# Pacing the side queue of a fused attention and feed-forward kernel: a constant number of queued jobs a step, gaps that end a step, and a later place for a partner's transposes

## The chip, the cores and the metric

The kernel runs on one core of one Trainium2 chip. The metric is the device time in microseconds (us). Each run is one execution of the whole program; runs of two kernels are compared on the same chip.

## The reference

Attention with root-mean-square normalised queries and keys, then a two-layer feed-forward block with a squared ReLU. All data are float32 (the weights arrive as float64 words).

```python
batch, n_heads, seq, head_dim = (8, 12, 448, 64)
n_tokens, d_model, d_ff = (3584, 768, 2048)

def rmsnorm(x, g):
    rms = np.sqrt(np.mean(x * x, axis=-1, keepdims=True) + 1e-06)
    return x / rms * g
q_n, k_n = rmsnorm(q, g_q), rmsnorm(k, g_k)
scores = 1.0 / np.sqrt(head_dim) * np.matmul(q_n, k_n.transpose(0, 1, 3, 2))
scores = scores - np.max(scores, axis=-1, keepdims=True)
attn = np.exp(scores)
attn = attn / (np.sum(attn, axis=-1, keepdims=True) + 1e-09)
x = np.matmul(attn, v)                  # (B, H, S, D)
x = x.transpose(0, 2, 1, 3).reshape(batch * seq, n_heads * head_dim)
h = np.maximum(x @ w_in, 0.0)
out = h * h @ w_out
```

## The kernel before

**Work and units.** The 96 heads are 48 pairs of two heads, six pairs to a batch element; the code numbers them i = 0 to 47. The feed-forward block runs over two batch elements at a time, so there are four units, `ffn(0)` to `ffn(3)`. Its products are formed with sums of blocks (fewer products, more additions): `first_products` (L961) in the first unit, `deep_products` (L995) in the others, and `second_products` (L1148) in all. While the products of a unit run on TensorE (PE), the attention of the pairs for the next unit is laid between them. The pairs up to 12 have no products beside them (`visit_alone`).

**Streams, steps and places.** `ffn` is a generator: each `yield` ends a step and gives its cost. Costs are 18 for a first product (6 matrix instructions), 30 or 10 in the second products of the first unit (4 instructions for 10), and 9 or 6 for deep products and 10 or 20 for second products later. `run(until)` (L1504) takes steps from the stream until the sum of costs, `spent`, reaches a place that `place(u, x)` gives. Then a visit to a pair follows. In the first unit a pair has two visits (`visit_among`, here called 14.0 and 14.1 for pair 14), 83.67 cost units apart. From pair 25 on a pair has one visit (`visit_whole`), at the places 99, 321 and 451 of each block of 481 units. Pair 25 is visited after the first unit has been drained, pair 37 after the second.

**What a visit does.** On PE it multiplies weights and values of the pair before (`attend`) and scores of this pair (`score`); ScalarE (ACT) makes exponentials from the scores (`weigh`, L453). An even pair's last score, `score(i, NJ)`, uses the transposed q and k of pair i + 1 also, its partner. All engines work through their instructions in the order of issue, which is the order in which this program's Python code runs.

**The side queue.** Small jobs that must be done between visits stand in two queues, `tasks` and `pool_tasks`. At the end of each step `run` calls `run_tasks(most, ...)`, with most = 2 for a cost above 10 and 1 otherwise; `run_tasks` (L1523) takes `most + len(some) // 5` jobs from the front of each queue. A visit begins with `run_all`, which empties both. In the later units some stretches of a block hold a queue back (`held`). The jobs are:

- for a coming pair, put in by `prepare` (L1665): room for squares; for x = 0 (q) and x = 1 (k), `square` (L172, ACT, into the same room) and `rows.add` (L191, a sum on VectorE, DVE, at L193 and a scaling at L196); then `put_in_order`, whose `rescale` runs on GpSimd (POOL: a power at L203, and a scaling of q at L218), with `store_q` and `load_blocks` (L325), which bring q, and k, back by blocks of 32 through DRAM;
- for the next pair, put in half way between two visits: `turn_blocks(i + 1, x)` (L363), a DVE transpose at L366 and, for q, a scaling on ACT at L368; and `load_qk(i + 4)`;
- after a visit: `invert`, `finish` or `invert_both` (divisions by the sums of weights, on DVE and POOL), and in `pool_tasks` six additions of weights (`add_up`, L472, POOL).

A `lambda: None` in the queue takes up the place of one job. In odd whole visits, jobs that were made by `partial` for this i (the turns of pair i + 1 and the load) are taken out before `run_all` as `late`, and put back to the front of the queue after the visit.

**Beside it.** In the same steps, `make_sum` (L1426) makes forms of the weights in turn on DVE and POOL (L1432), `convert` makes float32 weights from words (ACT L1319 to L1321, DVE L1332 to L1356), `deep_steps` derives and stores forms (L1392, L1410), and `follow_plan` makes forms of the attention's results (L718). DMAs of pairs go through a list, `transfers`, of which some are issued in each step (`follow_transfers`), all on the queue of SyncE (SP). When not in the first unit, `run_all` issues all that are left. `load_piece` (L879) brings in_sb, the weights of the deep products, from in_deep.

Of the kernel before, what the change touches and what calls it, by code (L numbers as in the profile page):

```python
# [224 lines left out]
def program(ctx, tc, rows, v, g, wide, ones, moe_w_in, moe_w_out, out, shift):  # L225
# [78 lines left out]
    def in_blocks(i):  # L304

        return 1 < i < len(pairs) and not alone(i - 2) and not shift
# [14 lines left out]
    def follow_transfers(most):  # L321
        for _ in range(min(len(transfers), most)):
            key, to, some = transfers.popleft()
            if to is not None:
                nc.sync.dma_start(to, some)  # L325
# [6 lines left out]
    def store_q(i):  # L332

        if not i % 2:
            through[i // 2] = dram.tile([2, S, 2 * D], F32, name="q_rows", tag="q_rows", bufs=2)
        to, queue = through[i // 2], transfers_of("q", i)
        queue.dma_start(
            to[i % 2, 0 : NJ * P].rearrange("(j p) c -> p j c", p=P),
            rows.part(i, 0)[:, 0:NJ].rearrange("p j h d -> p j (h d)"),
        )  # L340
        if not i % 2:
            for odd in range(2):
                queue.dma_start(
                    to[odd, NJ * P : S],
                    rows.room(i)[ds(odd * D, D), 0, NJ].rearrange("p h d -> p (h d)"),
                )

    def load_blocks(i, x):
        b, c = pairs[i]
        if x == 0 and slowly:  # L350
            while any(some[0][0] == "q" for some in list(transfers)[-4:]):
                transfers.append((("blocks", i, x), None, None))
        for e in range(2):
            source = through[i // 2][i % 2, :, ds(e * D, D)] if x == 0 else rows.qk[1][b, 2 * c + e]
            for half in range(2):
                transfers_of("blocks", i, x).dma_start(
                    room_for_blocks(i, x)[ds(e * D + half * SIDE, SIDE)].rearrange(
                        "p (t n) -> p t n", n=SIDE
                    ),
                    source[:, ds(half * SIDE, SIDE)].rearrange("(t p) n -> p t n", p=SIDE),  # L360
                )
# [26 lines left out]
    def rescale(i, x):  # L388
        ensure("qk", i)
        rows.power(i, x)  # L390
        if x == 0 or shift:
            rows.scale(i, x, nc.gpsimd)
# [20 lines left out]
    def new_weights(n, e):  # L413

        i, m = n
        if m < 2 and alone(i) and not shift:
            weights[n, e] = new_acc()[:, 0:S] if m else new_part()
        else:
            weights[n, e] = att.tile([P, S], F32, name="wT", tag="wT", bufs=8)
        return weights[n, e]  # L420

    def banks_of(i, m):

        if whole(i) and not shift:
            return [banks[n][:, 0:S] for n in ((0, 1), (2, 0), (1, 2), (0, 4))[m]]
        return [banks[m % 2 * 2 + e][:, 0:S] for e in range(2)]
# [23 lines left out]
    def weigh(i, m):  # L450

        for e, sc in enumerate(banks_of(i, m)):
            nc.scalar.activation(  # L453
                new_weights((i, m), e), sc, AF.Exp,
                scale=rows.rr[i][:, 1, 2 * m + e : 2 * m + e + 1],
            )
# [60 lines left out]
    def attend(i, some):  # L517

        order = values_of(i)
        for n in (i, i + 1 if joint(i) and i % 2 == 0 else i):
            ensure("v", n)
        for n in some:
            m = order[n]
            if joint(i):
                if m == NJ:
                    attend_both(i)
                else:  # L530
                    attend_halves(i, n)
                continue
            mine = ds(i % 2 * LASTS, LASTS) if m == NJ and shift else ds(0, P)
            for e in range(2):
                nc.tensor.matmul(  # L535
                    values_bank(i)[ds(e * D, D), :],
                    lhsT=lasts[i % 2][mine, e, :] if m == NJ else values[i][:, m, e, :],
                    rhs=weights[key_of(i, m), e][mine], start=n == 0, stop=n == len(order) - 1,
                )
# [67 lines left out]
    def both_denominators(i):  # L607

        for n in range(4):
            nc.tensor.matmul(  # L610
                sums_bank(i)[ts(n, SIDE), :], lhsT=ones[:, 0:SIDE],
                rhs=sums.pop((i + n // 2, n % 2)), start=True, stop=True,
            )
        take_sums(i)
# [838 lines left out]
    def follow_loads():  # L1453
# [17 lines left out]
    late = deque(  # L1471
        block + 2 + every * (n - 2 * tile_pieces) for n in range(len(all_pieces) - ahead)
    )
# [11 lines left out]

    VISITS, last, free_bank = 2, len(pairs) - 1, 1
    unit = 2 * NPAIR * VISITS
    tasks, pool_tasks, held = deque(), deque(), set()

    def place(u, x):  # L1490

# [10 lines left out]
    stream, spent, first, slowly = iter(()), COST, True, False  # L1502
# [19 lines left out]

    def run_tasks(most, to_send=0):  # L1523
        for name, some in (("others", tasks), ("pool", pool_tasks)):
            for _ in range(0 if name in held else min(len(some), most + len(some) // 5)):
                some.popleft()()
        follow_transfers(to_send)

    def run_all():
        before = set(held)  # L1530
        held.clear()
        while tasks or pool_tasks:
            run_tasks(len(tasks) + len(pool_tasks))
        if not first:
            follow_transfers(len(transfers))
        held.update(before)
# [28 lines left out]
    def square(i, x, room, engine=None):  # L1565
        if i <= last:
            ensure("qk", i)
            ensure("qk", i - i % 2)
            rows.square(i, x, room[:, 0 : 4 * P], engine)
# [7 lines left out]
    def weigh_slots(i, n):  # L1577
        if not shift:
            for m in slots_of(i, n):
                score(i, m)  # L1580
                weigh(i, m)
        elif n:
            weigh_shifted(i)

    def attend_all(i):
        slots = range(NJ + 1)
        attend(i, slots)
        add_weights(i, slots)
        forget(i, slots)
        take_sums(i)  # L1590
        invert(i)
        finish(i)
# [39 lines left out]
    def put_in_order(i):  # L1632
        for x in range(2):
            rescale(i, x)
        if in_blocks(i):
            steps = [lambda: store_q(i), lambda: load_blocks(i, 0)]
            for step in steps:
                tasks.extend((lambda: None, lambda: None, step))
# [26 lines left out]
    def prepare(i):  # L1665

        if i > last:
            return
        room = []
        tasks.append(  # L1670
            lambda: room.append(io.tile([P, 4 * P], F32, name="squares", tag="squares", bufs=1))
        )
        for x in range(2):
            tasks.append(lambda x=x: square(i, x, room[0]))
            if not first:
                tasks.append(lambda: None)
            tasks.append(lambda x=x: rows.add(i, x))
        tasks.append(lambda: pool_tasks.append(lambda: put_in_order(i)))
        if in_blocks(i):
            tasks.append(lambda: load_blocks(i, 1))  # L1680

    def visit_whole(i):
        late = [some for some in tasks if i % 2 and getattr(some, "args", None) == (i,)]
        for some in late:
            tasks.remove(some)
        run_all()
        if shift:
            attend_all(i - 1)
            if i <= last:
                weigh_slots(i, 1)  # L1690
        else:
            if i % 2 == 0:
                both_denominators(i - 2)
            for n in range(NJ):
                attend(i - 1, (n,))
                forget(i - 1, (n,))
                if i <= last:
                    score(i, n)
                    weigh(i, n)
            if i % 2:  # L1700
                attend(i - 1, (NJ,))
                forget(i - 1, (NJ,))
            join_halves(i - 1)
            if i % 2 == 0:
                tasks.append(lambda: invert_both(i - 2))
                if i <= last:
                    score(i, NJ)
                    weigh(i, NJ)
            if i <= last:
                additions(i)  # L1710
        tasks.extendleft(reversed(late))
        if shift or i % 2:
            prepare(i + 3)
        else:
            tasks.append(lambda: tasks.append(lambda: prepare(i + 3)))
        if i <= last:
            tasks.appendleft(lambda: load_v(i))
# [7 lines left out]
    with tc.manual_schedule(engines=ENGINES):  # L1725
# [8 lines left out]
        for i in range(len(pairs) + 1):  # L1734
            for n in range(1 if whole(i) else VISITS):
# [21 lines left out]
                if x == unit:  # L1757
                    drain()
                    stream, spent, first = ffn(u + 1), 0, u < 0
# [44 lines left out]
```

## Time and profile before

| What | Value |
| --- | --- |
| median of 3 runs | 1425.24 us (1421.85 to 1431.42) |
| profiled execution, its own time | 1425.5 us |
| its span, first to last instruction | 1423.4 us |
| mean granted PE clock | 0.993 |
| PE busy | 1377.7 us, 97% |
| weight loads (PEld) busy | 850.8 us, 60% |
| DVE / ACT / POOL busy | 841.4 / 587.6 / 784.3 us |
| first unit, with its visits | about 137 to 516 us |
| whole visits, 25 to 48 | 516.0 to 1150.2 us |

In the profile a line such as "PE bank L445 <- ACT qT L368" says that PE stood idle before an instruction of line 445 until the one of line 368 on ACT had ended. PEld is the load of the stationary operand, which overlaps the products. Lines of time have the start in us from the span's start, the duration in us, the engine, the line, the operation, what it writes and reads, and in brackets the idle time of the engine before it with what ended it.

### The profile page before, as it was taken

Reading aid. Unit: us, or ns where it says so; the run is one execution under the profiler, and the core shown is the slowest. Engines: PE = TensorE matmul, PEld = TensorE weight load, DVE = VectorE, ACT = ScalarE, POOL = GpSimd, SP = SyncE. Lnnn points to the kernel's source line nnn. Section 1 sums busy time; section 2 is a strip of 40 time slices with the busy share of each in tenths; the row PEclk is TensorE's granted clock in tenths of the full one; section 3 lists DMA queues with packets and bytes.
Section 4 is the critical chain, followed back from the end, with each engine's and each line's share of the span. In section 5 each row is a group of like instructions: output and inputs, shape, how many; then the busy total and the mean of one; then the engine's idle time right before and its main releaser. Section 6 shows DMA issues by size and latency. Waiting matters only on the chain.

```text
span 1423.4 us, 19419 instructions
## 1 busy us (share of the span) xinstructions
PE 1377.7 (97%) x6336; PEld 850.8 (60%) x6336; DVE 841.4 (59%) x1675; ACT 587.6 (41%) x1126; POOL 784.3 (55%) x778
## 2 busy tenths in 40 slices
PE   7998999989899999999999999999999999999998
PEld 3333444434344467585776758566675858778694
DVE  4997567877877775355455665445544565254444
ACT  6775456645546234433342434444243403221230
POOL 5666755564645696465485777655673554030311
PEclk9999999999999999999999999999999999999999
DMA  5555745966768957373654747465551716234132
GB/s 147 142 152 157 202 106 143 258 171 180 205 181 244 272 149 242 73 233 90 194 153 153 222 108 229 131 190 137 151 164 27 276 57 243 108 106 174 45 145 80
DMA packets 378931, 229.15 MB, mean 161 GB/s; under 512 B 271940, under 2 KB 347588, under 8 KB 374724
## 3 DMA queue, kind: packets, MB, share of 16 engines
q1 hardware_dynamic: 378528, 227.75, 55.2%
q8 instruction: 52, 0.85, 0.2%
q14 instruction: 59, 0.48, 0.1%
q10 hardware_dynamic: 292, 0.07, 0.0%
HBM read 172.49 MB, written 55.25 MB: 160 GB/s over the span
## 4 chain that ended last, share of the span: by engine, by line
PE 63%; POOL 3%; DVE 2%; DMA 2%; issue 2%; SPq 1%; ACT 1%; DVEq 0%; POOLq 0%; ACTq 0%
PE bank L1202 25%; PE bank L1024 20%; PE bank L1140 5%; PE bank L549 4%; PE bank L434 4%; PE bank L445 2%; PE bank L970 1%; POOL sum L472 1%; PE bank L535 1%; DMA in_sb<-in_deep 1%; PE bank L610 1%; PE bank L570 1%; DMA out_sb<-out_forms 0%; DVE acc L1259 0%; SPq L325 0%
## 5 line engine op out<-in xcount | busy, mean ns | idle before, releaser
L1024 PE MATMUL bank<-xT,in_sb 128*128 128x224 f32 x1344 | 289.5, 354 | 5.1 <-DMA in_sb<-in_deep 2.8
L1202 PE MATMUL bank<-out_sb,hid 128*128 128x384 f32 x768 | 271.0, 489 | 7.5 <-DVE acc L1259 5.8
L1259 DVE TENSOR_TENSOR acc<-acc,bank 128x384 f32<-128x384 f32 x324 | 173.0, 548 | 157.4 <-PE bank L1202 137.7
L1024 PEld LDWEIGHTS bank<-xT,in_sb 128*128 128x128 f32 x1344 | 252.4, 190 | 17.6 <-ACT wT L453 5.6
L453 ACT ACTIVATE wT<-bank,rr 128x448 f32<-128x448 f32 x288 | 164.1, 631 | 137.3 <-PE bank L434 74.3
L1202 PEld LDWEIGHTS bank<-out_sb,hid 128*128 128x128 f32 x768 | 144.5, 190 | 113.1 <-DVE acc L1259 9.8
L1202 PE MATMUL bank<-out_sb,sums 128*128 128x384 f32 x576 | 206.1, 490 | 1.7 <-DVE acc L1259 1.5
L203 POOL TENSOR_TENSOR rr<-ms,minus_half 128x8 f32<-128x8 f32 (+1 forms) x96 | 149.3, 1555 | 99.9 <-DVE ms L196 98.5
L1009 DVE TENSOR_TENSOR hid<-hid,bank 128x224 f32<-128x224 f32 x312 | 111.4, 384 | 87.8 <-PE bank L1024 83.5
L1202 PEld LDWEIGHTS bank<-out_sb,sums 128*128 128x128 f32 x576 | 107.7, 190 | 86.3 <-issue 4.2
L970 PE MATMUL bank<-xT,in_sb 128*128 128x448 f32 x336 | 131.9, 546 | 0.0
L472 POOL TENSOR_TENSOR sum<-sum,wT 128x448 f32<-128x448 f32 (+1 forms) x96 | 111.7, 1182 | 18.8 <-ACT wT L453 17.0
L1077 POOL TENSOR_TENSOR hid<-hid 128x448 f32<-128x448 f32 x24 | 27.4, 1141 | 160.2 <-DVE hid L1009 156.2
L445 PE MATMUL bank<-qT,kT 64*128 64x448 f32 (+1 forms) x492 | 107.1, 585 | 8.5 <-ACT qT L368 3.8
L472 POOL TENSOR_TENSOR sum<-wT 128x448 f32<-128x448 f32 x48 | 57.7, 1225 | 103.7 <-ACT wT L453 103.7
L970 PEld LDWEIGHTS bank<-xT,in_sb 128*128 128x128 f32 x336 | 62.1, 190 | 69.0 <-issue 62.5
L1140 PE MATMUL bank<-out_sb,hid 128*128 128x384 f32 x256 | 88.8, 493 | 0.0
L1081 ACT ACTIVATE hid<-hid 128x448 f32<-128x448 f32 x96 | 55.0, 573 | 75.3 <-DVE hid L1009 51.8
L193 DVE TENSOR_REDUCE ms<-squares 128x8 f32<-128x512 f32 (+1 forms) x68 | 41.8, 615 | 64.5 <-ACT squares L180 64.5
L445 PEld LDWEIGHTS bank<-qT,kT 64*128 64x128 f32 (+1 forms) x492 | 36.7, 170 | 71.1 <-issue 40.4
L1024 PE MATMUL bank<-more,in_sb 128*128 128x224 f32 x288 | 75.2, 355 | 3.2 <-DVE hid L1009 1.8
L434 PE MATMUL bank<-qT,kT 64*64 64x448 f32 x552 | 76.1, 541 | 0.8 <-ACT wT L453 0.8
(135 smaller groups left out, 2012.0 us busy)
## 6 DMA issues: line engine op xcount, KB each, us to landing
out_sb<-out_forms SPq DMA_DIRECT2D x24, 1536.0 KB, 9.7
in_sb<-in_deep SPq DMA_DIRECT2D x64, 384.0 KB, 3.8
in_sb<-in_deep SPq DMA_DIRECT2D x80, 256.0 KB, 4.1
words<-in_moe_w_in_dram SPq DMA_DIRECT2D x32, 384.0 KB, 3.7
words<-in_moe_w_out_dram SPq DMA_DIRECT2D x32, 384.0 KB, 3.5
out_forms<-out_sb SPq DMA_DIRECT2D x8, 1536.0 KB, 6.2
qk<-in_q_dram SPq DMA_DIRECT2D x96, 96.0 KB, 2.6
qk<-in_k_dram SPq DMA_DIRECT2D x96, 96.0 KB, 2.6
```

The costliest lines, as they stand in the source:

```text
L203: self.nc.gpsimd.tensor_tensor(out=self.rr[i][:, x, 0 : self.count(i)], in0=ms, in1=self.minus_half.to_broadcast(list(ms.shape)), op=ALU.pow,)
L434: nc.tensor.matmul(sc[ds(half * D, D)], lhsT=turned[i, 1][ds(e * D, D), ds(m * P + half * D, D)], rhs=turned[i, 0][ds(e * D, D), :], start ...
L445: nc.tensor.matmul(sc[some], lhsT=turned[p, 1][r, keys], rhs=turned[p, 0][r, :], start=True, stop=True,)
L453: nc.scalar.activation(new_weights((i, m), e), sc, AF.Exp, scale=rows.rr[i][:, 1, 2 * m + e : 2 * m + e + 1],)
L472: nc.gpsimd.tensor_tensor(out=sums[i, e][some], in0=left[some], in1=weights[key_of(i, m), e][some], op=ALU.add)
L549: nc.tensor.matmul(bank[ds(e * D, D), :], lhsT=values[i][keys, n, e, :], rhs=weights[(i, n), e][keys], start=n == 0, stop=n == NJ - 1 and ...
L970: nc.tensor.matmul(ps, lhsT=w_sb[:, IN.index(left), c, :], rhs=forms[u, c][right], start=first and c == 0, stop=c == NK - 1, skip_group_ch ...
L1009: nc.vector.tensor_tensor(out=quarter(name, n), in0=quarter(base, n), in1=ps, op=ALU.add)
L1024: nc.tensor.matmul(ps, lhsT=left, rhs=right, start=start, stop=stop, skip_group_check=True)
L1140: nc.tensor.matmul(ps, lhsT=hid[a].rearrange("p t e s -> p t (e s)")[:, t, ds(NT * P, P)], rhs=w_sb[t][:, 2 * a + half, :], start=(a, t) = ...
L1202: nc.tensor.matmul(ps, lhsT=lefts[left][:, t, ts(tt, P)], rhs=w_sb[t][:, OUT.index(right), :], start=first and t == 0, stop=t == 1, skip_g ...
L1259: nc.vector.tensor_tensor(out=acc, in0=acc, in1=ps, op=ALU.add)
```

## The change

It has three parts.

1. In the first unit (`first` true) a step takes exactly `most` jobs from each queue, however many stand there.
2. A named job, `gap`, ends the work of the step on the queue that it stands in. In the later units it takes the place of the empty job between a square and its sum; for even pairs another follows each sum; and when jobs of `late` are put back after a visit, three gaps stand before them.
3. `late` is now taken out in even visits also. There its jobs run inside the visit, after the score and the weights of n = 1, and nothing is put back.

```diff
-    tasks, pool_tasks, held = deque(), deque(), set()
+    tasks, pool_tasks, held, gap = deque(), deque(), set(), lambda: None
...
     def run_tasks(most, to_send=0):
         for name, some in (("others", tasks), ("pool", pool_tasks)):
-            for _ in range(0 if name in held else min(len(some), most + len(some) // 5)):
-                some.popleft()()
+            for _ in range(0 if name in held else most if first else most + len(some) // 5):
+                if not some:
+                    break
+                task = some.popleft()
+                task()
+                if task is gap:
+                    break
         follow_transfers(to_send)
...
         for x in range(2):
             tasks.append(lambda x=x: square(i, x, room[0]))
             if not first:
-                tasks.append(lambda: None)
+                tasks.append(gap)
             tasks.append(lambda x=x: rows.add(i, x))
+            if not first and i % 2 == 0:
+                tasks.append(gap)
...
     def visit_whole(i):
-        late = [some for some in tasks if i % 2 and getattr(some, "args", None) == (i,)]
+        late = [some for some in tasks if getattr(some, "args", None) == (i,)]
         for some in late:
             tasks.remove(some)
         run_all()
...
                 if i <= last:
                     score(i, n)
                     weigh(i, n)
+                while n == 1 and i % 2 == 0 and late:
+                    late.pop(0)()
...
         tasks.extendleft(reversed(late))
+        if late:
+            tasks.extendleft([gap] * 3)
         if shift or i % 2:
             prepare(i + 3)
```

## The prediction

> **What bounds the kernel now.** I read the page first: PE is busy 97% of 1423.4 us, so whatever the change does must show in the 3% that is left, or in the clock. The change moves no matrix product: its queued jobs issue to ScalarE, VectorE, GpSimd and the DMA queue only, and PE's order in a visit stays as it is. So the next view is the busy time by stretch. The columns are the stretch, its length, busy us with instruction counts for PE, PEld, DVE, ACT and POOL, PE's granted clock, DMA share and GB/s. The first two stretches are the first unit and the two units with whole visits; the change touches nothing before 137 us or after about 1150 us.
>
> ```profile
> 137.00:516.00 379.00, 364.88 (x1196) 166.36 (x1189) 278.11 (x483) 196.09 (x377) 229.41 (x192) 0.99 0.70 190
> 516.00:1150.00 634.00, 623.94 (x3377) 434.29 (x3376) 328.92 (x687) 246.33 (x466) 407.21 (x440) 1.00 0.55 161
> 372.53:375.94 3.41, 0.96 (x6) 0.19 (x4) 3.38 (x7) 2.99 (x7) 1.30 (x2) 1.00 1.12 299
> 375.94:379.36 3.42, 3.42 (x8) 1.51 (x5) 3.28 (x6) 2.88 (x7) 3.34 (x4) 0.50 0.92 270
> 478.34:481.76 3.42, 1.25 (x4) 0.30 (x2) 1.70 (x3) 0.00 (x0) 3.26 (x4) 1.00 1.07 353
> 481.76:488.58 6.82, 5.78 (x14) 1.88 (x16) 4.21 (x7) 0.00 (x0) 6.40 (x7) 0.50 0.80 226
> ```
>
> PE idles 14.1 us in the first unit (379.0 less 364.9) and 10.1 us in the next two. That is all there is to win, but for one thing: twice a window of 3.4 us in which PE idled 2.45 us and 2.17 us is followed by half clock, for 3.4 us and 6.8 us, which costs 1.7 and 3.4 us more. So 14.1 + 10.1 + 5.1 = 29.3 us is the ceiling. The waits of PE in these two stretches (us in total, times, longest), first unit first:
>
> ```profile
> PE bank L1202 <- DVE acc L1259: 7.3, 6, 2.2
> PE bank L445 <- ACT qT L368: 3.8, 2, 2.5
> PE bank L1202 <- POOL out_sb L1432: 1.8, 1, 1.8
> ...
> PE bank L1024 <- DMA in_sb<-in_deep: 2.8, 2, 1.7
> PE bank L1024 <- DVE hid L1009: 2.7, 4, 0.8
> PE bank L1024 <- ACT part L1013: 2.3, 4, 0.6
> PE bank L1024 <- DVE hid L1019: 1.4, 3, 0.5
> ```
>
> PE waits for VectorE that comes late, directly or by way of ScalarE's scaling of qT. Why is it late? VectorE's own order of time ahead of PE's longest wait in a visit (second visit of pair 20; start, us, what, and in brackets the idle time before it), and that wait in PE's:
>
> ```profile
> 364.32 0.69 DVE L193 TENSOR_REDUCE ms<-squares 128x8 f32<-128x512 f32 x1 [1.06 <-ACT squares L180]
> ...
> 366.76 0.69 DVE L193 TENSOR_REDUCE ms<-squares 128x8 f32<-128x512 f32 x1 [0.80 <-ACT squares L180]
> ...
> 374.17 0.64 DVE L366 STREAM_TRANSPOSE qT<-qk 128x448 f32<-128x448 f32 x1
> ```
> ```profile
> 375.56 1.42 PE L445 MATMUL bank<-qT,kT 64*64 64x448 f32 x4 [2.45 <-ACT qT L368]
> ```
>
> From 364.3 us on VectorE has no idle time except the 0.80 us; it runs behind, and the transpose that PE needs stands behind all of it. It lost 1.06 + 0.80 us to a sum of squares issued in the same step as the squares it sums. Over the first unit these waits are 44.2 us in 18 places (VectorE's waits there, first row), over the whole visits 18.4 us in 12. Most are harmless; the reader is to see that they matter where no slack follows. GpSimd late in the first unit:
>
> ```profile
> 474.23 2.62 POOL L472 TENSOR_TENSOR sum<-wT 128x448 f32<-128x448 f32 x2
> 476.93 1.33 POOL L472 TENSOR_TENSOR sum<-sum,wT 64x448 f32<-64x448 f32 x1
> 478.34 1.02 POOL L1432 TENSOR_TENSOR out_sb<-out_sb 128x384 f32<-128x384 f32 x1
> 479.44 2.36 POOL L472 TENSOR_TENSOR sum<-sum,wT 64x448 f32<-64x448 f32 x2
> 481.76 0.99 POOL L1432 TENSOR_TENSOR out_sb<-out_sb 128x384 f32<-128x384 f32 x1
> ```
>
> Five additions of weights that nobody waits for stand ahead of the weight form (481.76) that PE waits 1.76 us for.
>
> **What the Trainium skill says.** "TensorE: Matmul & The Clock Gate", Part 1, states a free-running window of 3413 ns and a halved clock after an idle one; the trace agrees (3.42 and 6.82 us at 0.50), though a window with 1.25 us of work was enough. "Perfetto Trace Analysis", Tensor Engine Instruction, has ACT, DVE and GPSIMD as strict FIFO: a sum waiting for its squares holds up all that stands behind it, as at 366.76. "SBUF — State Buffer", Who interferes with whom, says a DVE operation with two SBUF inputs is blocked by a GpSimd operation that reads SBUF; L1392 takes 0.55 us at 372.64 and 1.24 us at 374.73 beside GpSimd. "DMA: Bandwidth & Descriptors", Anatomy of one DMA, puts every semaphore wait of a DMA on the issuing sequencer, so a store that waits on SP delays the loads after it.
>
> **The change part by part.** I walked the queue by hand from visit to visit with the step costs 18, 30, 10 (first unit) and 9, 9, 9, 6, 10, 20.
>
> *Constant rate.* With most at 2 (cost 18 or 30) or 1 (cost 10), the queue loses the extra task it had when five or more stood in it. In a first visit, run_tasks(2) now issues the room and the first squares; their sum comes a step later. With 18-steps the order was: squares 0 and sum 0 in the visit, squares 1 and sum 1 in step 1, the rescale in step 2. It becomes: squares 0 | sum 0 | squares 1 and sum 1 | rescale. With 10-steps all four are apart and the sums come two steps later. So every sum of x = 0 stops waiting, and the x = 1 sums still share a step with their squares where steps cost 18. The turn of qT keeps its place in VectorE's order in the 18-intervals (end of the last step and start of the visit are the same place), and comes one step, 4 products or 1.29 us, earlier in the 10-intervals. Of the six additions after a visit, 2 instead of 3 are issued in the 30-step. The store of q, its reload by blocks and the load of k by blocks go one or two steps later, and the store and q's reload now fall into the second visit's run_all; q's turns are over 150 cost units away, so that is hidden.
>
> Place by place. Visit 18.1: PE waits 1.35 us for qT; the turn is issued 1.29 us earlier and VectorE lost 3.72 us to a sum just before: -1.35 (0 to -1.35). Visit 20.1: of 1.86 us lost to sums about 1.0 comes back, because the second pair waits for ScalarE later; PE's 2.45 us becomes 1.6. A window with 1.89 us idle (290.6 to 294.0) was not followed by half clock, so 1.6 should not be: -0.8 and -1.7 (0 to -4.2). After visit 17.1: 4.5 us of waits for VectorE, which is busy throughout; it is again about 0.9 less behind: -0.9 (0 to -2). After visit 23.1: one addition fewer, 1.1 us, ahead of the weight form, and 0.3 from VectorE: -1.4; the half clock (3.4) goes if the window's idle falls from 2.17 to about 1.5, which I count at half: -1.7 (0 to -6.8 in all).
>
> Against it: at the unit's end eight 10-steps no longer empty the queue, and both turns of pair 26 are issued by the drain, directly ahead of visit 25. There PE already waits 0.81 us for ScalarE; two products' additions (0.54 us each) now stand before the turns: +1.0 (0 to +4 with a half clock). The rescale's 0.83 to 1.04 us of GpSimd moves closer to the second products' start and slows VectorE's two-input work beside it, and the sum of x = 1 waits there instead: four blocks at 0.6, +2.5 (0 to +5).
>
> *Gaps.* In whole visits each sum gets a step of its own. At 617 us VectorE's second sum (0.54 + 0.17 us) stands between two hid additions and PE waits 0.61 us behind it; it goes a step on, three times: -1.8. The 0.85 us at 796.9 goes likewise: -0.85. The 0.53 to 0.62 us for ScalarE's part, four times, stay: ScalarE is held there by squares that wait for GpSimd, not by a sum. Three gaps ahead of an odd visit's turns move two transposes (0.64 us each) three 10-steps on, into stretches without a PE wait: nothing. The queue reloads in another order around the two waits for in_sb (1.71 and 1.06 us), where SP issues some 15 loads of 0.5 us first: -0.7 (0 to -2.8).
>
> *The turn inside even visits* concerns pairs 30, 36 and 42 alone, the only ones with a turn left over. It takes 0.63 us of VectorE and 0.67 us of ScalarE from ahead of the visit to the middle. PE loses 0.15 us there now (6.78 against 6.63 us), and the last score needs the turn some 2 us later: nothing either way, at worst +0.5 each.
>
> Sum: -1.35 - 2.5 - 0.9 - 3.1 + 1.0 + 2.5 - 1.8 - 0.85 - 0.7 = -7.7 us. The profiled execution took 1425.5 us (2.1 us around its span), as good as the median of 1425.24: 1417.8, say 1418.
>
> **The rivals.** *Only the waits change places* (1423 to 1428, taken as 1425): VectorE is full from 364 to 380 us and waits later instead. For it: the x = 1 sums still share a step. Against it: visit 18.1. *All of it comes* (1406 to 1411): every item at its far end, clock included, gives -15 or more. *k's blocks land too late* (1428 to 1440, taken as 1432): the load of k by blocks goes a step, 2.3 us, later, behind the nine in_deep loads at the start of the last second products. Before visit 24.0 VectorE already idles 1.81 us for it (481.88), with PE's additions queued behind. It decides once the blocks land over 1 us later than now; three transitions at up to 3 us, and a half clock each of 1.7, make up to +14, against the gains of -7.7 a net +6. Against it: elsewhere the blocks land 4 us or more ahead (281.8 issued, wanted at 292.4).
>
> **How the numbers follow.** The forecast 0.50 (own range 1412 to 1423), waits change places 0.22, all of it 0.10, late blocks 0.18. Leaving out the ends of the last two gives 1408 to 1433. About 1% (14 us) is what a measurement here tells from no change: faster by that needs nearly every item (0.10), slower the far end of the late blocks (0.05).
>
> **What would show it.** Right: no wait at visit 18.1; under 1.7 us at visit 20.1 and full clock after it; additions of sums issued between weight forms; VectorE's wait for squares well under 44 us; no 0.61 us wait three times before odd visits. Wrong: the wait before visit 25 over 3 us; VectorE waiting for k's blocks in second products; new waits for in_sb; a half clock in other places.

## The result, and the profile after

| | before | after |
| --- | --- | --- |
| median of the runs beside each other (5 each; the table ahead of the prediction has the first three of before) | 1425.24 us | 1415.96 us (1414.36 to 1417.75) |
| ratio, 95% interval | | 0.993 (0.9912 to 0.9948) |
| span of the profiled execution | 1423.4 us | 1414.6 us |
| start of visit 14.0 to start of visit 26 | 391.7 us | 385.0 us |
| start of visit 26 to start of the visit after pair 47 | 610.4 us | 609.5 us |

The kernel is 9.3 us faster (0.7%), and 8.8 us of it are seen between the two profiled executions: 6.7 us from visit 14.0 to visit 26, 0.9 us in the whole visits, and 1.2 us ahead of visit 14.0, where the change reaches nothing (a half clock at 113 us lasted 6.8 us in before's execution, one at 114 us 3.4 us in the other). The forecast of 1418.0 lay 2 us too high. Nearly all of what the change can have done is in the first unit, with the boundary at its end. By stretch, first the two stretches that are set against those of before (the cut at 510.4 us lies inside visit 25, which begins at 505.4 us here and at 516.0 us in before), then the window with the wait of visit 20.1 and the window after it, the two around visit 25, and one at 285 us that will be needed later:

```profile
137.00:510.40 373.40, 361.71 (x1214) 165.72 (x1212) 281.00 (x486) 197.60 (x380) 232.00 (x195) 1.00 0.72 194
510.40:1141.00 630.60, 623.45 (x3348) 434.05 (x3348) 331.75 (x682) 243.87 (x465) 403.24 (x436) 1.00 0.56 161
367.04:370.45 3.41, 2.65 (x14) 0.51 (x10) 2.63 (x6) 2.91 (x6) 0.99 (x1) 1.00 0.94 270
370.45:373.87 3.42, 3.41 (x12) 1.78 (x13) 3.12 (x3) 3.32 (x7) 3.26 (x4) 1.00 0.92 211
506.96:510.37 3.41, 1.68 (x16) 0.43 (x8) 2.20 (x5) 1.08 (x2) 3.33 (x4) 1.00 0.40 90
510.37:513.79 3.42, 3.25 (x20) 1.25 (x24) 0.00 (x0) 1.80 (x4) 3.15 (x4) 0.50 0.38 88
285.13:288.54 3.41, 1.74 (x6) 0.54 (x4) 3.41 (x5) 1.55 (x3) 2.77 (x4) 1.00 0.73 169
```

PE still idles 11.7 us in the first stretch (373.4 less 361.7), of which 1.8 us are part of the wait in visit 25. From the start of visit 14.0 to the start of visit 26 it idles 11.8 us instead of 14.9. The window at 367 us idles 0.76 us where its like in before idled 2.45, and the clock after it is whole. The half clock at 482 us is gone too. One is new, at 510.4 us, behind the wait of visit 25.

PE's waits, in the first unit and (below the dots) in the whole visits; columns as before, us in total, times, longest:

```profile
PE bank L1202 <- DVE acc L1259: 4.9, 5, 1.5
PE bank L601 <- ACT wT L453: 3.0, 3, 1.3
PE bank L445 <- ACT qT L368: 0.8, 1, 0.8
PE bank L1202 <- POOL out_sb L1432: 0.7, 1, 0.7
...
PE bank L1024 <- ACT part L1013: 2.4, 4, 0.6
PE bank L434 <- ACT wT L453: 1.9, 1, 1.9
PE bank L1024 <- DMA in_sb<-in_deep: 1.6, 1, 1.6
PE bank L1024 <- DVE hid L1009: 1.5, 3, 0.7
PE bank L1024 <- DVE hid L1019: 1.5, 3, 0.5
```

Against before, 7.3 became 4.9, 3.8 became 0.8 and 1.8 became 0.7. The denominators' wait (L601) rose from 1.0 to 3.0; its line in before is

```profile
PE bank L601 <- ACT wT L453: 1.0, 3, 0.4
```

VectorE's order of time ahead of visit 20.1 shows why the wait for qT shrank (start, us, what, and in brackets its idle time), with the wait itself on PE below:

```profile
360.91 0.69 DVE L193 TENSOR_REDUCE ms<-squares 128x8 f32<-128x512 f32 x1
...
364.40 0.69 DVE L193 TENSOR_REDUCE ms<-squares 128x8 f32<-128x512 f32 x1 [0.52 <-ACT squares L180]
...
369.07 0.64 DVE L366 STREAM_TRANSPOSE qT<-qk 128x448 f32<-128x448 f32 x1
```
```profile
370.46 0.97 PE L445 MATMUL bank<-qT,kT 64*64 64x448 f32 x4 [0.77 <-ACT qT L368]
```

The first sum finds its squares ready. The second waits 0.52 us where the pair of them lost 1.86 us before. Over the first unit VectorE's wait for squares fell from 44.2 us in 18 places to 20.4 us in 11 (before, then after):

```profile
DVE ms L193 <- ACT squares L180: 44.2, 18, 5.8
DVE ms L193 <- ACT squares L180: 20.4, 11, 3.4
```

GpSimd ahead of the weight form that PE waits for after visit 23.1:

```profile
467.79 2.60 POOL L472 TENSOR_TENSOR sum<-wT 128x448 f32<-128x448 f32 x2
470.36 1.31 POOL L1432 TENSOR_TENSOR out_sb<-out_sb 128x384 f32<-128x384 f32 x1
471.74 2.41 POOL L472 TENSOR_TENSOR sum<-sum,wT 64x448 f32<-64x448 f32 x2
474.23 0.99 POOL L1432 TENSOR_TENSOR out_sb<-out_sb 128x384 f32<-128x384 f32 x1
```

Four additions stand there instead of five, and PE waits 0.69 us instead of 1.76.

### The profile page after: what moved, and what is told of

It reads as the page before. It is cut to its first block, busy times and chain, and to the rows that moved or that the text cites. A ratio compares the mean times of both kernels' runs of the same rounds, so it can differ in the third digit from the quotient of the medians.

```text
span 1414.6 us, 19459 instructions
## 1 busy us (share of the span) xinstructions
PE 1374.7 (97%) x6336; PEld 850.2 (60%) x6336; DVE 846.8 (60%) x1675; ACT 586.7 (41%) x1126; POOL 784.1 (55%) x778
## 4 chain that ended last, share of the span: by engine, by line
PE 77%; DVE 5%; POOL 5%; DMA 4%; issue 3%; ACT 3%; SPq 3%; POOLq 0%; DVEq 0%; ACTq 0%
PE bank L1202 29%; PE bank L1024 20%; PE bank L1140 5%; PE bank L970 5%; PE bank L434 4%; PE bank L549 4%; PE bank L445 4%; PE bank L535 3%; POOL sum L472 2%; DMA words<-in_moe_w_in_dram 1%; SPq L317 1%; PE bank L610 1%; PE bank L601 1%; ACT wT L453 1%; PE bank L570 1%
## 5 line engine op out<-in xcount | busy, mean ns | idle before, releaser
L203 POOL TENSOR_TENSOR rr<-ms,minus_half 128x8 f32<-128x8 f32 (+1 forms) x96 | 147.8, 1539 | 82.1 <-DVE ms L196 66.9
L1009 DVE TENSOR_TENSOR hid<-hid,bank 128x224 f32<-128x224 f32 x312 | 111.1, 383 | 85.8 <-PE bank L1024 81.9
L549 PE MATMUL bank<-wT,vt 64*64 64x448 f32 x576 | 75.1, 550 | 0.0
```

The source lines that it names most:

```text
L203: self.nc.gpsimd.tensor_tensor(out=self.rr[i][:, x, 0 : self.count(i)], in0=ms, in1=self.minus_half.to_broadcast(list(ms.shape)), op=ALU.pow,)
L549: nc.tensor.matmul(bank[ds(e * D, D), :], lhsT=values[i][keys, n, e, :], rhs=weights[(i, n), e][keys], start=n == 0, stop=n == NJ - 1 and ...
L1009: nc.vector.tensor_tensor(out=quarter(name, n), in0=quarter(base, n), in1=ps, op=ALU.add)
```

## The experiments

The theory after this comparison: the constant rate carries the gain, by way of VectorE's sums and of the half clock; gaps and the turn are worth next to nothing. Its rivals were that the whole visits carry it, or that it is chance which windows fall to half clock.

### Each part alone

Rate alone, put into the kernel before:

```diff
-            for _ in range(0 if name in held else min(len(some), most + len(some) // 5)):
+            more = 0 if first else len(some) // 5
+            for _ in range(0 if name in held else min(len(some), most + more)):
```

> The kernel before with only part 1 of the change: in the first unit a step takes exactly `most` jobs from each queue. Theory (the first unit carries the gain): VectorE's sums no longer wait for squares and one addition fewer stands ahead of the weight form, so PE idles some 4 us less between 137 us and visit 25, the half-clock windows at 376 and 482 us go, and the boundary visit 25 pays 1.1 us and one half clock (1.7 us); the median is 6 to 8 us below before, whole units unchanged (three waits of 0.61 us on hid L1009 still there). Rival (the whole units carry it): at most 3 us below before. Rival (chance: which windows fall to half clock decides): the first unit's waits go as in the changed kernel, but the half-clock windows stand elsewhere and the time is within 3 us of before.

Measured: 1413.46 us (1412.49 to 1417.00), before beside it 1424.93, ratio 0.9911 (0.9897 to 0.9924). The first unit carries it. Of the three waits of 0.61 us on hid L1009 nothing changed, as expected. In the profiled execution the half-clock windows at 376 and 482 us are gone, as expected, but two others fell to half clock, at 288 us (6.8 us long) and at 514 us (3.4 us), and cost as much together as the two of before. It was the slowest of the five (1417.0 us) and still 8 us below before: which windows fall does not explain the gain by itself. The gain was 11.5 us, larger than expected; see the repetition below.

Gaps alone: the job `gap`, its break and the three gaps ahead of late jobs, with the old rate and `late` taken out in odd visits only.

> The kernel before with only part 2: the gap job ends a step's work in the later units (between square and sum, after each sum of even pairs, three of them ahead of an odd visit's late jobs). Theory (the first unit carries the gain): the first unit stays as before with both half-clock windows; the three waits of 0.61 us on hid L1009 ahead of visits 28, 34 and 40 go, waits for in_sb change by a us either way: 1.5 to 2.5 us below before. Rival (the whole units carry it): 5 us or more below before.

Measured: 1425.68 us, ratio 1.0006 (0.9996 to 1.0016). No gain, so the rival of the whole visits falls, and my own 1.5 to 2.5 us as well. PE's waits in its whole visits:

```profile
PE bank L1024 <- DVE hid L1009: 1.5, 3, 0.8
PE bank L1024 <- DVE hid L1019: 1.4, 3, 0.5
PE bank L1024 <- DMA in_sb<-in_deep: 1.1, 2, 0.6
```

The waits for L1009 do fall, from 2.7 to 1.5 us. The three of 0.61 us are gone, but a new one of 0.39 us stands some 14 us on in two of the three places (633.32 and 961.61 us), and the one of 0.85 us is still 0.76. The interval leaves at most 0.6 us of gain, so these 1.2 us do not show in the time. The first unit kept both half-clock windows of before, as expected, and this execution has one more, at 289 us.

The turn alone: `late` taken out in even visits too, and run after the score and weights of n = 1.

> The kernel before with only part 3: late jobs of even visits (pairs 30, 36 and 42) run inside the visit after the score and weights of n = 1. Theory (the turn costs a little): the visits 30, 36 and 42 become 6.9 us long instead of 6.6 to 6.8, 0.3 us each, so 0.5 to 1 us above before. Rival (the turn inside the visit is a gain because VectorE and ScalarE are free ahead of the visit): 0.5 us or more below before.

Measured: 1424.89 us, ratio 0.9998 (0.9989 to 1.0008): nothing in the median. In the profile the even visits 30, 36 and 42 last 6.90, 6.92 and 6.92 us instead of 6.60, 6.78 and 6.59, together 0.8 us more. The last score of visit 30, first before, then with the turn alone, and ScalarE's scaling with the turn alone:

```profile
660.85 1.15 PE L445 MATMUL bank<-qT,kT 64*64 64x448 f32 x8
```
```profile
659.20 1.45 PE L445 MATMUL bank<-qT,kT 64*64 64x448 f32 x8
```
```profile
658.96 0.67 ACT L368 ACTIVATE qT<-qT,g 128x448 f32<-128x448 f32 x1
```

The scaling ends at 659.63 us, 0.43 us after the score began. The eight products take 0.3 us longer.

Rate and gaps without the turn:

> The changed kernel without part 3: rate and gaps, late jobs taken out in odd visits only. Theory (the turn costs a little): visits 30, 36, 42 at 6.6 to 6.8 us, 0.5 to 1 us below the changed kernel, so 9 to 10.5 us below before. Rival (the turn gains, or keeps the sums and turns apart): 0.5 us or more above the changed kernel, with a new wait ahead of visits 30, 36 or 42.

Measured: 1416.70 us (1413.55 to 1418.09), ratio 0.9931 (0.9916 to 0.9946), within the noise of the changed kernel. The three visits are back at 6.59, 6.78 and 6.60 us, but a wait of 2.17 us for in_sb at 880.6 us is there in this execution.

### Which queue carries it

The constant rate on `tasks` alone, and on `pool_tasks` alone:

```diff
-            more = 0 if first else len(some) // 5
+            more = 0 if first and name == "others" else len(some) // 5
```

> The kernel before with the constant rate in the first unit on `tasks` (others) alone; `pool_tasks` keeps its extra jobs, so three of the six additions of weights are issued in the 30-step as before. Theory (VectorE's sums carry the gain; the pool pacing both gives and takes): waits at visits 18.1 and 20.1 as small as with the whole rate (0 and 0.8 us), the denominators' waits back at 0.37 us in the first and third block (-1.9 us against the whole rate, since GpSimd's third addition again fills its idle time ahead of the hidden sums), the wait for the weight form after visit 23.1 back at about 1.8 us (+1.1 us): 1411 to 1415, and up to 1417 if the half clock at about 480 us comes back. Rival (the pool pacing carries the gain): 1420 or more. Rival (the denominators' longer wait comes from the later sums on VectorE): it stays at 1.3 us here.

> The kernel before with the constant rate in the first unit on `pool_tasks` alone; `tasks` keeps its extra jobs. Theory (VectorE's sums carry the gain): waits at visits 18.1 and 20.1 stay at 1.35 and 2.45 us with the half clock after 20.1, denominators wait 1.3 us in the first and third block (+1.9), the weight form after visit 23.1 comes 1.1 us sooner and its half clock may go (-1.1 to -4.5): 1421 to 1426. Rival (the pool pacing carries the gain): 1417 or less.

Measured: `tasks` alone 1415.71 us, ratio 0.9925 (0.9905 to 0.9946); `pool_tasks` alone 1423.54, ratio 0.9985 (0.9974 to 0.9995). VectorE's jobs carry the gain; the additions add a little at most. PE's waits in the first unit, `tasks` alone, then `pool_tasks` alone:

```profile
PE bank L1202 <- DVE acc L1259: 5.8, 5, 2.2
...
PE bank L1202 <- POOL out_sb L1432: 1.8, 1, 1.8
PE bank L601 <- ACT wT L453: 1.0, 3, 0.4
PE bank L445 <- ACT qT L368: 0.8, 1, 0.8
```
```profile
PE bank L1202 <- DVE acc L1259: 6.7, 7, 1.5
PE bank L445 <- ACT qT L368: 3.8, 2, 2.5
PE bank L601 <- ACT wT L453: 3.0, 3, 1.3
...
PE bank L1202 <- POOL out_sb L1432: 0.7, 1, 0.7
```

The wait for qT goes with `tasks`; the weight form's wait and the longer wait of the denominators go with `pool_tasks`. The latter is not an effect of the sums, then. The half clock that was expected after visit 20.1 with `pool_tasks` alone did not come in the profiled execution, and no other window of the two stretches fell to it (see the clock's share, below). GpSimd in before, and in the kernel after, ahead of the first of the longer waits:

```profile
248.01 3.30 POOL L472 TENSOR_TENSOR sum<-sum,wT 128x448 f32<-128x448 f32 x3 [4.60 <-ACT wT L453]
256.18 1.28 POOL L1126 TENSOR_TENSOR sums<-hid 128x384 f32<-128x384 f32 x1 [4.87 <-ACT hid L1112]
```
```profile
247.10 2.23 POOL L472 TENSOR_TENSOR sum<-sum,wT 128x448 f32<-128x448 f32 x2 [4.06 <-ACT wT L453]
255.27 1.29 POOL L1126 TENSOR_TENSOR sums<-hid 128x384 f32<-128x384 f32 x1 [5.94 <-ACT hid L1112]
256.51 2.54 POOL L472 TENSOR_TENSOR sum<-sum,wT 64x448 f32<-64x448 f32 x2
...
262.79 1.30 POOL L1126 TENSOR_TENSOR hid<-hid 128x384 f32<-128x384 f32 x1
```

Before, the third addition ran in GpSimd's idle time. Paced, it runs between the hidden sums, and these come later. The last of them then lies over VectorE's L1332, before and after:

```profile
263.94 0.35 DVE L1332 TENSOR_SCALAR out_sb<-words 128x384 uint32<-128x384 uint32 x1
264.21 0.61 DVE L1110 TENSOR_TENSOR hid<-bank,part 128x448 f32<-128x448 f32 x1
```
```profile
263.16 1.15 DVE L1332 TENSOR_SCALAR out_sb<-words 128x384 uint32<-128x384 uint32 x1
264.23 0.61 DVE L1110 TENSOR_TENSOR hid<-bank,part 128x448 f32<-128x448 f32 x1
```

The Trainium skill, "SBUF — State Buffer", Who interferes with whom, says that a tensor_scalar on VectorE can take the ports that it shares with GpSimd and that one of the two then blocks wholly. Which of the two blocks, the page leaves to the order of issue; so the prediction's "is blocked by" holds where GpSimd began first, as it did in that place of before (374.56 us, ahead of L1392 at 374.73) and does here (262.79 us, ahead of L1332 at 263.16). The trace agrees: 1.15 us beside the hidden sum, 0.35 us without. It is not so each time: over the fourteen profiled executions L1332 took 0.31 to 0.37 us in the 267 places with no GpSimd instruction beside it, and 0.32 to 2.39 us in the 451 that lay wholly beside one. In the order of the engines the hidden value of L1110 then waits behind it, ScalarE's weights behind that, and PE at the denominators 1.31 us instead of 0.37. That the additions' pace causes the longer wait is shown by the two kernels; the steps between are read from the traces.

Yet this costs nothing in sum. In the `tasks` kernel the denominators wait 0.38 us, and the next long wait, 23 us on, is 2.17 us (290.79) instead of 1.23. In the third block the 0.92 us go into the weight form's wait, 1.76 instead of 0.69. What PE is ahead at one place it loses at the next that VectorE or GpSimd sets.

### The boundary

The constant rate only up to visit 24.1, so that the turns of pair 26 are issued ahead of the drain again, and the same with `tasks` alone:

```diff
-            more = 0 if first else len(some) // 5
+            more = 0 if first and spent < COST * 23 / 24 else len(some) // 5
```

> The kernel before with the constant rate from the start of the first unit up to visit 24.1 only; after that the old rate, so that the queue is empty at the drain and both turns of pair 26 are issued two steps earlier, as before. Theory (the boundary costs 1.1 us and a half clock because the turns fall into the drain): the wait at visit 25 falls from 1.9 to 0.8 us and full clock after it: 1 to 2.8 us below the constant rate alone (1413.5), 1410.5 to 1412.5. Rival (the wait at visit 25 is set by PE coming sooner, not by the turns): still 1.9 us there, 1413 to 1414.

> Both: the constant rate on `tasks` alone and only up to visit 24.1. Theory: denominators 0.37 us (-1.9), boundary 0.8 us and full clock (-1.1 to -2.8), weight form after visit 23.1 1.8 us (+1.1), half clock there open (0 to +3.4): 1409 to 1413. Rival (the parts don't add up, since PE's lead is taken back at the next wait): not below the better of its two parts.

Measured: 1415.95 us (1413.57 to 1419.00), ratio 0.993 (0.9909 to 0.9951), and 1416.45 (1413.50 to 1421.26), ratio 0.9928 (0.9903 to 0.9952). The wait at visit 25 is gone in both (0.1 us at most, where 0.8 was expected), so the rate after visit 24.1, and with it the turns in the drain, did cause it; but the median doesn't fall. In the profiled execution with `tasks` alone, which took 1420.14 us, the stretch after the boundary reads:

```profile
548.10:551.52 3.42, 0.72 (x4) 0.37 (x2) 0.39 (x2) 3.22 (x8) 2.05 (x3) 1.00 0.76 227
551.52:558.34 6.82, 6.10 (x14) 4.59 (x15) 1.24 (x3) 0.88 (x2) 3.81 (x4) 0.50 0.98 344
```

PE came sooner to the deep products and waited 3.42 us for in_sb, and half clock followed.

### Repetitions, and one attempt on in_sb

Rate alone, the changed kernel and the rate up to visit 24.1 once more, beside each other, and a fourth kernel: the rate up to 24.1 in which a visit of the later units issues half of the pair transfers that are left, not all.

```diff
-            follow_transfers(len(transfers))
+            follow_transfers(len(transfers) // 2)
```

> The constant rate alone once more, beside the changed kernel. If gaps and turn are worth nothing (their waits only change places, plus 0.8 us for the turn): within 1 us of the changed kernel, or up to 1 us below. If they cost: 2 us or more below the changed kernel again, as in the first run of it (1413.5). Its profile shows which waits differ between two executions of one kernel: the half-clock windows and the waits for in_sb should, the waits for VectorE and ScalarE should not by more than 0.1 us.

> The changed kernel once more. The waits for VectorE, ScalarE and GpSimd in the first unit repeat within 0.1 us; the half clock at visit 25 (1.9 us of waiting) may or may not come; the waits for in_sb at about 550 and 880 us vary by a us or more. Median 1414 to 1418.

> The constant rate up to visit 24.1 once more, beside the constant rate alone. Theory (what the boundary wins is taken back where PE comes to in_sb before it has landed): no wait at visit 25, a wait for in_sb at about 548 us of 0.5 to 3 us, and a median within 1 us of the constant rate alone. Rival (the boundary's gain is kept): 1.5 us or more below it.

> The constant rate up to visit 24.1, and in the later units a visit issues only half of the pair transfers that are left, so that loads of in_sb come sooner on SP's queue. Theory (the in_sb waits come from the pair transfers ahead of them on SP): the waits at about 548 and 878 us fall to under 0.5 us, 1 to 2 us below the constant rate up to visit 24.1. Rival (in_sb is late by the DMA engines' load, not by SP's order): the waits stay, same time within 1 us; or pair transfers come late and a visit waits for its qT: 1 us or more above.

| beside before at 1426.05 us | median us | lowest to highest | ratio, 95% |
| --- | --- | --- | --- |
| rate alone | 1417.21 | 1414.08 to 1417.84 | 0.9933 (0.9916 to 0.9950) |
| changed kernel | 1416.59 | 1415.97 to 1418.92 | 0.9940 (0.9924 to 0.9957) |
| rate up to visit 24.1 | 1416.98 | 1412.58 to 1420.86 | 0.9943 (0.9923 to 0.9964) |
| the same, half the transfers | 1417.44 | 1415.76 to 1419.91 | 0.9945 (0.9929 to 0.9961) |

The four can't be told apart, and the lead that rate alone had in its first run did not repeat. PE's waits in the whole visits, rate up to 24.1 and then half the transfers:

```profile
PE bank L1024 <- DMA in_sb<-in_deep: 2.2, 1, 2.2
```
```profile
PE bank L434 <- DVE inverse L643: 3.9, 1, 3.9
```

With half the transfers no wait for in_sb is left in this execution. That agrees with SP's order setting it but does not show it: the changed kernel's second execution, with all transfers issued, has none either. And visit 26 then waits 3.9 us, behind a transpose of VectorE. VectorE's own order of time has the reason: its transpose of q at 529.99 us waited 5.88 us for q's reload (qk from q_rows), one of the pair transfers that now go out late. It is no better.

The repetition gave something else. The changed kernel's second execution, windows at 286 and 511 us with what follows each:

```profile
285.76:289.17 3.41, 1.74 (x5) 0.59 (x4) 3.27 (x6) 1.13 (x3) 2.85 (x3) 1.00 0.73 179
289.17:295.99 6.82, 5.82 (x14) 1.94 (x12) 5.33 (x9) 1.55 (x3) 3.17 (x3) 0.50 0.70 254
511.08:514.50 3.42, 1.58 (x20) 0.77 (x24) 0.56 (x2) 2.80 (x5) 3.34 (x5) 1.00 0.19 58
514.50:517.90 3.40, 3.40 (x26) 2.22 (x18) 0.62 (x1) 2.69 (x6) 3.32 (x4) 1.00 0.54 95
```

The waits of the first unit are the same as in the first execution within 0.05 us, save two (1.00 for 1.23 us, and 0.30 us at 166.75 that is missing here). In the two executions of rate alone the wait of 1.23 us was 0.65 and 0.93 us, more apart than the 0.1 us expected. But here the window with 1.67 us idle at 286 us is followed by 6.8 us of half clock, where the first execution's, also with 1.67 us (285.13 above), was not. And the one at visit 25, with 1.84 us idle, is followed by full clock, where the first execution's 1.73 us was followed by half.

### The clock's share

How long a window at half clock lasts can be read for each profiled execution. From the start of visit 14.0 to the start of visit 26, in us, with half of the time at half clock counted as lost:

| profiled execution | length | PE idle | lost to half clock |
| --- | --- | --- | --- |
| before | 391.7 | 14.9 | 5.1 |
| changed kernel, first and second | 385.0, 385.2 | 11.8, 11.3 | 1.7, 3.4 |
| rate alone, first and second | 387.2, 385.3 | 11.0, 11.3 | 5.1, 3.4 |
| `tasks` alone | 385.1 | 11.8 | 1.7 |
| `pool_tasks` alone | 387.9 | 15.2 | 0 |
| rate up to visit 24.1, first and second | 381.0, 381.1 | 9.8, 9.9 | 0, 0 |

So the first unit's gain of 6.7 us in the changed kernel is 3.1 us of idle time and 3.4 us of clock, and what `pool_tasks` alone gained there was clock. The mean granted clock of every other execution is on record too. An estimate from it (the share that was not granted times the span, which counts half clock anywhere in the program): before lost 10.3 us in the mean of 73 executions, the changed kernel 5.5 us in 11. About half of the gain of 9 us is thus clock. Within the kernels, the times of all 189 executions go with this loss (correlation 0.80).

## Why the prediction was right, and where its steps were wrong

The time came out near the forecast for its first reason, VectorE's sums in the first unit, but with terms that were off on both sides. The first unit gave 2.4 us more than forecast and the whole visits 2.5 us less (0.9 us in the profiled execution, 3.35 forecast); that these cancel is luck.

**First unit.** Counted from 137 us to the start of visit 26, gains and costs of my list sum to -4.35 us; measured, visit 14.0 to visit 26 takes 385.0 us instead of 391.7, which is -6.7, and in the other executions with the whole rate and its end unchanged 384.7 to 387.2.
- Visit 18.1: -1.35 forecast, -1.35 measured; the wait is gone.
- Visit 20.1: -0.8 forecast, -1.7 measured. I had counted 1.0 us back of the 1.86 us that VectorE lost to its sums; 1.34 came back, and the transpose came still earlier than that. Its half clock went, -1.7 as said.
- After visit 17.1: -0.9 forecast. These waits fell from 4.6 to 2.9 us, but 0.94 of that had been paid at the denominators 20 us earlier: -0.8 over both.
- After visit 23.1: -1.4 forecast for the waits; they fell from 3.45 to 1.39 us, 2.06, of which 0.94 again were paid at the denominators before: -1.1. The half clock of 3.4 us, which I had counted at half, went wholly.
- Boundary: +1.0 forecast for the wait, +1.08 measured (0.81 to 1.89), and a half clock of 1.7 us, which I had named as the far end, in one of the two executions.
- The term of +2.5, "four blocks at 0.6", is the step that failed in its cause. Extra waits came, 2.0 us at the denominators, but from the third addition on GpSimd and not from the rescale or a late sum; and they are taken from waits that follow. (The rescale's 0.83 to 1.04 us was also short: in before L218 takes 0.83 to 1.46 us, and the power at L203 another 1.3 to 2.0.) Without this term my sum for the unit is -6.85, against -6.7. That is close partly by luck: the half clock after visit 23.1 gave 1.7 us more than counted and the one at the boundary took 1.7 us, and larger gains at single waits stand against the losses at the denominators.

**Gaps.** -1.8 and -0.85 forecast: the step that failed in size. I followed a sum to the step from which it was taken and not to the one where it landed; gaps alone took 1.2 us of waits away and moved the median by nothing. The 0.85 us stayed, 0.76. The waits for in_sb, -0.7 forecast, show no effect of the change: they were 0 to 4.6 us in the fourteen profiled executions, 1.65 and 0 in the two of the changed kernel.

**The turn in even visits.** "Nothing either way" was wrong by 0.8 us over three visits, inside the "+0.5 each" that I had set as the worst. ScalarE has room in the visit on average, but its scaling stands in the order between two sets of weights.

**Rivals.** "Only the waits change places" is true of the additions and of the boundary, not of the sums. "k's blocks land too late" did not happen: VectorE's wait for them rose from 6.7 to 8.2 us (ahead of visit 24.0 from 1.8 to 3.2), and no wait of PE for them or behind them appeared.

**A window with 1.89 us idle.** I took from one window of before that 1.6 us idle are safe. They are not, as the last section shows; the forecast held because the windows that fall to half clock became fewer, not because they were excluded.

**What stays open.** The rate up to visit 24.1 has a wide spread. Both of its profiled executions were the fastest of their six, with no half clock in the two stretches. Its slow ones lose clock: by the estimate above, the three slow executions of its second run (1419.2 to 1420.9 us) lost 8.5 to 9.9 us, the three fast ones (1412.6 to 1414.8 us) 2.8 to 5.7. Which waits bring that on is not shown; the 3.4 us for in_sb with half clock behind it, in the kernel with `tasks` alone, is a guess at it. No kernel here was shown to beat the changed one.

## What to carry to other kernels

Where side work is issued in the order of the engines' queues, put a step between a producer on one engine and its consumer on another: it is the consumer's wait at the head of the queue that costs, and only where nothing slack follows. Follow a moved job to where it lands as well as from where it left, on every engine that it is moved past; an addition that filled idle time is no longer free when it is paced. And judge a wait that is taken away by the next wait of the same engine, since a lead is kept only if nothing further on is bound to another stream. Last, read the granted clock of each execution beside its time: here it was about half of the gain, and most of the spread went with it.

## What the runs showed of the hardware

- The half clock needs no idle window. The Trainium skill, "TensorE: Matmul & The Clock Gate", Part 1, gives the clock as halved after one or more idle windows; here a window in which PE was busy for half of its 3.41 us was enough at times. Over the fourteen profiled executions, of the windows at full clock within the two stretches, all 9 with 1.91 us idle or more were followed by half clock, of 18 with 1.63 to 1.90 us 8 were, and none with less. (Idle is the length less PE's busy time, whose ends are modelled, so the edges are not sharper than that.) What decides between 1.63 and 1.90 us stays open: two windows with 1.67 us, at the same waits of the changed kernel, went different ways.
- The grid of these windows lies differently against the program in each execution, and a wait counts by how much of it falls into one window. The wait of 2.45 us in visit 20.1 lay in one window in before (2.45 us idle, half clock followed). In `pool_tasks` alone and in the turn alone the same wait (2.45 and 2.46 us) lay over the edge of two; the larger part made 1.68 and 1.57 us of idle time in its window, and full clock followed.
- Two executions of the changed kernel, with nearly the same waits, lost 1.7 and 3.4 us to half clock in the two stretches, at visit 25 in the one and at 286 us in the other. Both executions of the rate up to visit 24.1, which have no long wait at visit 25, lost nothing there. One profile of such a kernel is not its profile.
- A tensor_scalar of 128x384 on VectorE took 1.15 us beside a GpSimd addition and 0.35 us without; PE's wait behind it, at 268.3 us, was 0.94 us longer.
